# A new order of jobs on five engine queues, and other engines for some copies, squares and evacuations, in a gated recurrence fused with a feed-forward network

## The chip, the cores and the metric

The kernel runs on one core of a Trainium2 chip. The metric is the device time of one execution in microseconds (us); the runs shown give their median. The core has a matrix engine (PE, TensorE), three engines for elementwise work (VectorE or DVE, ScalarE or ACT, GpSimd or POOL) and a queue (SP) that issues the transfers. Each engine works through its own queue strictly in order and waits, through semaphores, for what its next instruction needs.

## The reference

A gated linear recurrence over 4 sequences of 5824 steps with 256 channels, and a feed-forward network on each of the 23296 tokens that it gives:

```python
sig_r = 1.0 / (1.0 + np.exp(-r_gate)); sig_i = 1.0 / (1.0 + np.exp(-i_gate))
log_a = c * sig_r * np.log(np.clip(a_base, 1e-06, 1.0 - 1e-06))[None, None, :]
a_t = np.exp(log_a)
norm = np.sqrt(np.maximum(1.0 - a_t * a_t, 1e-06))
x_gated = norm * sig_i * x
for t in range(S):
    h = a_t[:, t] * h + x_gated[:, t]
    y[:, t] = h
...
a = x @ w1          # x is y, 23296 x 256; w1, w2: 256 x 1024
b = x @ w2
h = a * b @ w3      # w3: 1024 x 1024
return (h @ w_out)  # w_out: 1024 x 256
```

## The kernel before

The tokens are cut into 47 chunks: 0 and 1 of 256 tokens, 2 to 45 of 512, and 46 of 256. The product of `w3` and `w_out` is formed once at the start, so that a chunk needs three matrix products: two up (256 to 1024) and one down (1024 to 256). The recurrence needs channels on the partitions and time along the row, so the gates are turned, in some chunks by PE, in the others by a transposing transfer.

Each chunk is a set of small jobs, and the program is one string, `ORDER`, of job names. A loop reads it word by word and calls the function that emits the job's instructions. Each engine's queue is therefore the string without the jobs of other engines; no scheduler moves anything afterwards. Eight sets of numbers (`DV_COPY`, `AC_SQUARE` and so on) say on which engine a copy, square, cast or evacuation is emitted. The buffers are rings: a job that takes the next buffer of a ring waits for the reader of its former content. The product `a` and the down product share a ring of four PSUM buffers.

The jobs, with `c` the chunk, and in brackets engine and line of the profile:

- `r i x`: loads of the two gates and of x (SP, L151); `L` and `C`: load and cast of a piece of a weight (L407; L414 or L416)
- `R I`: tanh of the gates (ACT, L160 to L168); `p`, `t`: gate plus one, and its product with x, the tile `u_t`, in two halves (POOL, or DVE at L189 or L192)
- `V U`: the turning of both (PE, L200, or SP, L211)
- `d`: exp, the decay `a_t`, one job for each half of the channels (ACT, L223); `s`: its square, into `nrm` (POOL or DVE L233, ACT L231); `q`: root (ACT, L238); `g`: product with the turned `u_t` (DVE, L248 or L251)
- `h`: the scan, one for each half of the channels (DVE, L270); `y`: cast to bf16 (POOL, L282)
- `a`, `b`: the up products into the tiles `pa` and `pb` (PE, L299). `a7.3.0` is chunk 7, group 3 of 4, first half; `b7.3` is both halves
- `c`: copy of `pa` from PSUM to `sa` (ACT L322 or DVE L320); `m`: product of `sa` and `pb` into `g_t` (DVE, L337)
- `D`: down product of 128 tokens, 8 matmuls over the groups of `g_t` in their order, into `po` (PE, L357); `e`: its evacuation to `ot` (ACT L322 or DVE L320); `o`: store (SP)
- `Ft Fc Fm Fe`: the forming of `w3` times `w_out`: turning (PE, `ptw`), copy of `ptw`, product (PE, `pw`), evacuation of `pw` (DVE L472 or ACT)
- `W`: two matmuls without use, to keep PE active (L287); `E`, `A`: small preparations.

A chunk's chain is loads, `R I`, `V U`, `d s q g`, `h`, `y`, `a b`, `c`, `m`, `D`, `e`, `o`. The recurrence of a chunk is computed some chunks ahead of its matrix products.

```python
    def copy_to(dve, dst, src_ps):
        if dve:
            nc.vector.tensor_copy(out=dst, in_=src_ps)
        else:
            nc.scalar.copy(out=dst, in_=src_ps)
...
    for word in ORDER.split():
        name, args = re.fullmatch(r"([LC]w[123o]\.|A\d\.|[A-Za-z]+)([\d.]*)", word).groups()
        steps[name](*(int(v) for v in args.split(".") if v))
```

Of the kernel before, what the change touches and what calls it, by code (L numbers as in the profile page):

```python
# [23 lines left out]
def kernel(  # L24
# [150 lines left out]
    def times(c, half):  # L175
# [49 lines left out]
    def square(c, cb):  # L225
# [6 lines left out]
        else:  # L232
            (nc.vector if (c, cb) in DV_SQUARE else nc.gpsimd).tensor_mul(out=n, in0=a, in1=a)  # L233

# [37 lines left out]
    def cast(c, cb=None):  # L272
# [8 lines left out]
        else:  # L281
            (nc.vector if key in DV_CAST else nc.gpsimd).tensor_copy(out=y, in_=h)  # L282

# [190 lines left out]
    def last(c):  # L474
# [33 lines left out]
        I7 I8 D0.1 D0.0 b3.0 b3.1 a3.1.0 g4 h4.0 h4.1 s5.1 R8 R9 d6.0 d6.1 p6 y4 p8 t5.0 t5.1 D0.3 D0.2 m3.0 e0.0
# [156 lines left out]
```

## Time and profile before

| what | before |
|---|---|
| time of the runs shown | 511.43 us median (511.33, 511.43, 511.6) |
| span of the profiled execution | 509.1 us (its own time is not listed; the median of the runs is 2.3 us above its span) |
| PE busy | 501.7 us, 99% of the span, 3225 matmuls |
| ScalarE busy | 461.5 us, 91% |
| VectorE busy | 431.8 us, 85% |
| GpSimd busy | 318.0 us, 62% |
| moved by transfers | 124.06 MB, mean 244 GB/s |
| granted PE clock | 1.000 |

Busy times are unions of the instructions' intervals. Matmuls overlap one another, so a matmul is read by the distance from its start to the next start and not by its length. An engine's row in the order of time gives start and length of a run of equal instructions, their count behind the x, and in brackets how long the engine stood idle before it and what ended that.

### The profile page before, as it was taken

Reading aid. Unit: us, or ns where it says so; the run is one execution under the profiler, and the core shown is the slowest. Engines: PE = TensorE matmul, PEld = TensorE weight load, DVE = VectorE, ACT = ScalarE, POOL = GpSimd, SP = SyncE. Lnnn points to the kernel's source line nnn. Section 1 sums busy time; section 2 is a strip of 40 time slices with the busy share of each in tenths; the row PEclk is TensorE's granted clock in tenths of the full one; section 3 lists DMA queues with packets and bytes.
Section 4 is the critical chain, followed back from the end, with each engine's and each line's share of the span. In section 5 each row is a group of like instructions: output and inputs, shape, how many; then the busy total and the mean of one; then the engine's idle time right before and its main releaser. Section 6 shows DMA issues by size and latency. Waiting matters only on the chain.

```text
span 509.1 us, 8891 instructions
## 1 busy us (share of the span) xinstructions
PE 501.7 (99%) x3225; PEld 308.3 (61%) x3225; DVE 431.8 (85%) x417; ACT 461.5 (91%) x708; POOL 318.0 (62%) x269
## 2 busy tenths in 40 slices
PE   7999999999999999999999999999999999999997
PEld 3767665665665656556656556565566655656566
DVE  6999999999999789879979799878877797959762
ACT  7999999998999999999999999998998979888543
POOL 1686677658658937964886973956647568580200
PEclk9999999999999999999999999999999999999999
DMA  8999999999989998896999997899886895252213
GB/s 317 410 411 345 335 316 282 305 286 259 310 220 298 279 285 247 211 302 196 247 305 327 254 286 148 252 243 227 210 246 164 235 298 161 85 166 62 65 51 104
DMA packets 178048, 124.06 MB, mean 244 GB/s; under 512 B 87378, under 2 KB 174036, under 8 KB 178004
## 3 DMA queue, kind: packets, MB, share of 16 engines
q1 hardware_dynamic: 178000, 123.50, 85.4%
q8 instruction: 25, 0.41, 0.4%
q14 instruction: 19, 0.16, 0.1%
q10 hardware_dynamic: 4, 0.00, 0.0%
HBM read 78.91 MB, written 23.86 MB: 202 GB/s over the span
## 4 chain that ended last, share of the span: by engine, by line
PE 92%; ACT 3%; DMA 2%; POOL 1%; DVE 1%; issue 1%; SPq 1%; ACTq 0%; DVEq 0%
PE po L357 30%; PE pb L299 29%; PE pa L299 29%; DMA wf<-in_moe_w_dram 2%; PE pw L436 1%; ACT sa L322 1%; PE ptr L200 1%; PE ptw L425 1%; POOL u_t L192 0%; DVE h_t L270 0%; SPq L151 0%; ACT ot L322 0%; SPq L407 0%; ACT L168 0%; ACT L238 0%
## 5 line engine op out<-in xcount | busy, mean ns | idle before, releaser
L337 DVE TENSOR_TENSOR g_t<-sa,pb 128x1024 bf16<-128x1024 bf16 (+1 forms) x188 | 218.7, 1180 | 58.9 <-PE pb L299 27.6
L299 PEld LDWEIGHTS <-w_sb 128*128 128x128 bf16 x1504 | 146.4, 98 | 144.1 <-issue 1.4
L322 ACT CAST sa<-pa 128x512 bf16<-128x512 f32 (+1 forms) x332 | 179.8, 591 | 27.1 <-PE pa L299 18.9
L299 PE MATMUL pa<-y_t,w_sb 128*128 128x512 bf16 (+1 forms) x752 | 190.2, 372 | 0.2 <-ACT sa L322 0.2
L299 PE MATMUL pb<-y_t,w_sb 128*128 128x512 bf16 (+1 forms) x752 | 184.9, 372 | 0.2 <-ACT w_sb L414 0.2
L357 PE MATMUL po<-wp_sb,g_t 128*128 128x256 bf16 (+1 forms) x1464 | 177.6, 272 | 0.0
L357 PEld LDWEIGHTS <-g_t 128*128 128x128 bf16 x1464 | 142.5, 98 | 39.5 <-issue 0.3
L282 POOL CAST y_t<-h_t 128x1024 bf16<-128x1024 f32 (+2 forms) x47 | 53.8, 1145 | 140.2 <-DVE h_t L270 136.1
L192 POOL TENSOR_TENSOR u_t<-i_t,x_t 128x512 bf16<-128x512 f32 (+1 forms) x90 | 123.3, 1387 | 3.8 <-DMA ut<-u_t 1.8
L270 DVE TENSOR_TENSOR_SCAN h_t<-a_t,h_t,nrm 128x512 f32<-128x512 f32 (+1 forms) x92 | 121.1, 1343 | 1.6
L233 POOL TENSOR_TENSOR nrm<-a_t 128x512 f32<-128x512 f32 x70 | 78.4, 1137 | 7.0 <-ACT a_t L223 4.0
L223 ACT ACTIVATE a_t<-rt,la 128x512 f32<-128x512 bf16 (+1 forms) x82 | 66.1, 823 | 0.0
L322 ACT COPY ot<-po 128x512 f32<-128x512 f32 x84 | 49.1, 589 | 13.2 <-PE po L357 12.9
L173 POOL TENSOR_SCALAR i_t<-i_t 128x1024 f32<-128x1024 f32 (+1 forms) x45 | 55.4, 1233 | 8.3 <-ACT i_t L168 8.3
L251 DVE SCALAR_TENSOR_TENSOR nrm<-nrm,ut 128x1024 f32<-128x1024 f32 (+1 forms) x39 | 53.2, 1365 | 5.2 <-ACT nrm L238 5.2
L168 ACT ACTIVATE i_t<-i_t 128x1024 f32<-128x1024 f32 (+1 forms) x46 | 48.5, 1063 | 0.3 <-DMA i_t<-in_i_gate_dram 0.2
L238 ACT ACTIVATE nrm<-nrm 128x1024 f32<-128x1024 f32 (+1 forms) x47 | 48.4, 1040 | 0.2
L162 ACT ACTIVATE th_r<-r_t 128x1024 bf16<-128x1024 f32 (+1 forms) x41 | 43.5, 1064 | 0.0
L320 DVE CAST sa<-pa 128x512 bf16<-128x512 f32 x36 | 23.5, 684 | 1.4 <-PE pa L299 0.8
L238 ACT ACT_TABLE_LOAD x17 | 21.8, 1283 | 0.4
L287 PE MATMUL warm<-ident 128*128 128x512 bf16 x32 | 10.7, 473 | 1.6 <-DVE ident L441 1.6
L231 ACT ACTIVATE nrm<-a_t 128x512 f32<-128x512 f32 x18 | 11.4, 645 | 0.0
(55 smaller groups left out, 122.1 us busy)
## 6 DMA issues: line engine op xcount, KB each, us to landing
r_t<-in_r_gate_dram SPq DMA_DIRECT2D x45, 512.0 KB, 5.2
i_t<-in_i_gate_dram SPq DMA_DIRECT2D x45, 512.0 KB, 6.0
x_t<-in_x_dram SPq DMA_DIRECT2D x45, 512.0 KB, 5.5
out_dram<-ot SPq DMA_DIRECT2D x90, 256.0 KB, 3.9
wf<-in_moe_w_dram SPq DMA_DIRECT2D x12, 512.0 KB, 10.5
wf<-in_moe_w_out_dram SPq DMA_DIRECT2D x2, 512.0 KB, 10.2
rt<-th_r SPq DMA_TRANSPOSE x41, 4.7
ut<-u_t SPq DMA_TRANSPOSE x39, 4.4
```

The source lines that it names most:

```text
L173: (nc.vector if c in DV_PLUS else nc.gpsimd).tensor_scalar(t, t, 1.0, 1.0, op0=ALU.add, op1=ALU.mult)
L192: (nc.vector if (c, half) in DV_HALF else nc.gpsimd).tensor_mul(out=u, in0=t, in1=xt)
L223: nc.scalar.activation(out=a, in_=pr, func=AF.Exp, scale=la4[:, cb:cb + 1], bias=la4[:, cb:cb + 1])
L233: (nc.vector if (c, cb) in DV_SQUARE else nc.gpsimd).tensor_mul(out=n, in0=a, in1=a)
L238: nc.scalar.activation(out=n, in_=n, func=AF.Sqrt, scale=-1.0, bias=1.0)
L251: nc.vector.scalar_tensor_tensor(out=n, in0=n, scalar=1e-3, in1=T["pu", c][:, :, cols], op0=ALU.max, op1=ALU.mult)
L270: nc.vector.tensor_tensor_scan(h[:, cb, :], a[:, cb, :], n[:, cb, :], init, ALU.mult, ALU.add)
L282: (nc.vector if key in DV_CAST else nc.gpsimd).tensor_copy(out=y, in_=h)
L299: nc.tensor.matmul(out=dst, lhsT=w_sb[:, cb, m * P:(m + 1) * P], rhs=T["y", gates_of(c)][:, cb, span(c, mp)], start=(cb == 0), stop=(cb == ...
L322: nc.scalar.copy(out=dst, in_=src_ps)
L337: nc.vector.tensor_mul(out=T["g", z][:, 2 * mp:2 * mp + 2, span(c, mp)], in0=T["sa", c, mp][:, :, :w], in1=T["pb", c, mp][:, :, :w])
L357: nc.tensor.matmul(out=po, lhsT=T["g", c][:, k, j * P:(j + 1) * P], rhs=wp_sb[:, k, cols], start=(k == 0), stop=(k == KD - 1), skip_group_ ...
```

## The change

All five queues get a new order up to about chunk 26; from there on the string is the old one word for word (PE from `a26.3.1`, VectorE from `h28.0`, ScalarE from `c26.3.0`, GpSimd from `s31.1`, SP from `o24.0`). The jobs are the same; the transposes that PE makes, the ring sizes and the number of warming matmuls stay. These jobs change their engine:

| job | before | after |
|---|---|---|
| copies `c` on VectorE (others ScalarE) | 36, all up to chunk 12 | 70: 37 up to chunk 12, 33 later |
| evacuations `e` on VectorE | 7 | 11: 5 up to chunk 12, 6 later |
| squares `s` on ScalarE | 18 | 29 |
| squares `s` on GpSimd | 70 | 59 |
| second product `t` of a half on VectorE (others GpSimd) | 0 | 3 |
| whole cast `y` on ScalarE (others GpSimd) | 0 | 2 |
| fold copies `Fc` and evacuations `Fe` on VectorE | 8 and 4 | 7 and 6 |
| weight cast `Cw1.1` | VectorE | GpSimd |
| cast of chunk 1 on VectorE and ScalarE | `y1.1` and `y1.0` | `y1.0` on VectorE, none on ScalarE |

```diff
-    DV_HALF = set()
-    DV_SQUARE = {(0, 0), (0, 1), (5, 1), (9, 0)}
+    DV_HALF = {(9, 1), (16, 0), (30, 1)}
+    DV_SQUARE = {(0, 0), (0, 1), (7, 0), (26, 1)}
...
-    DV_CAST = {(1, 1)}
-    AC_CAST = {(1, 0)}
+    DV_CAST = {(1, 0)}
+    AC_CAST = {22, 24}
...
-    DV_EVAC = {(0, 0), (0, 1), (4, 1), (5, 1), (6, 1), (9, 0), (9, 1)}
-    FOLD_ACT = {('e', 0), ('e', 4), ('e', 5), ('e', 7)}
+    DV_EVAC = {(0, 0), (0, 1), (4, 0), (5, 0), (7, 0), (14, 1), (17, 0), (19, 1), (20, 0), (22, 0), (23, 0)}
+    FOLD_ACT = {('c', 7), ('e', 6), ('e', 7)}
...
-    W_ACT = {('w2', 0), ('w3', 3)}
-    W_DVE = {('w1', 1)}
+    W_ACT = {('w2', 0), ('w3', 5)}
+    W_DVE = set()
...
     ORDER = """
-        r0 i0 x0 Lw1.1 Lw1.0 r2 i2 Lw2.0 Lw3.2 x2 E W13 A3. A0. A1. A2. R0.1 R0.0 W3 W10 V0.0 V0.1 I0 t0.1 d0.0 s0.0
+        r0 E W0 A3. A0. A1. A2. W11 W1 R0.1 V0.1 W7 i0 R0.0 V0.0 I0 x0 W3 t0.0 d0.1 Lw1.1 d0.0 Lw1.0 W4 W15 t0.1
...
-        a7.0.1 b7.1 c7.3.0 R15 c7.0.0 c7.0.1 D6.0 D6.1 a7.3.1 D5.0 D6.2 b7.3 D6.3 D5.1 d11.1 c7.3.1 e6.0 s11.1 I12
+        m7.1 p11 o4.0 r15 x12 r17 h8.0 d11.0 D6.1 h8.1 a7.3.1 D6.0 e6.0 c7.3.1 a7.0.0 c7.0.0 b7.3 o6.0 m7.3 D6.3
```

In the last pair of lines PE's jobs are, before, `b7.1 D6.0` with `a7.0.0 a7.0.1` ahead of them, and after, `b7.1` (on the line ahead) and `D6.1` with `a7.0.0` behind.

The first place is the start of VectorE's queue, from the products of chunk 0 (`u_t`) and squares (`nrm<-a_t`) through the first gatings (`nrm<-nrm,ptr`) and scans (`h_t`) to the first copies (`sa`) and products (`g_t`). Before:

```order
L189 SCALAR_TENSOR_TENSOR u_t_157<-i_t_99,x_t_101 128x512
L233 TENSOR_TENSOR nrm_161<-a_t_159 128x512 x2
L189 SCALAR_TENSOR_TENSOR u_t_157<-i_t_99,x_t_101 128x512
L416 CAST w1_sb_90<-wf_103 128x2x512
L248 SCALAR_TENSOR_TENSOR nrm_161<-nrm_161,ptr_182 128x256 x2
L270 SCALAR_TENSOR_TENSOR h_t_214<-a_t_159,nrm_161 128x256 x2
L248 SCALAR_TENSOR_TENSOR nrm_161<-nrm_161,ptr_182 128x256 x2
L270 SCALAR_TENSOR_TENSOR h_t_214<-a_t_159,h_t_214,nrm_161 128x256 x2
L282 CAST y_t_217<-h_t_214 128x256
L320 CAST sa_271<-pa_220 128x2x256
L320 CAST sa_273<-pa_223 128x2x256
L337 TENSOR_TENSOR g_t_278<-sa_271,pb_266 128x2x256
```

And the same stretch after:

```order
L194 SCALAR_TENSOR_TENSOR u_t_149<-i_t_135,x_t_144 128x512 x2
L238 TENSOR_TENSOR nrm_184<-a_t_151 128x512 x2
L253 SCALAR_TENSOR_TENSOR nrm_184<-nrm_184,ptr_169 128x256 x2
L275 SCALAR_TENSOR_TENSOR h_t_193<-a_t_151,nrm_184 128x256 x2
L253 SCALAR_TENSOR_TENSOR nrm_184<-nrm_184,ptr_169 128x256 x2
L275 SCALAR_TENSOR_TENSOR h_t_193<-a_t_151,h_t_193,nrm_184 128x256 x2
L287 CAST y_t_212<-h_t_193 128x256
L325 CAST sa_246<-pa_241 128x2x256
L325 CAST sa_259<-pa_250 128x2x256
L342 TENSOR_TENSOR g_t_268<-sa_259,pb_261 128x2x256
L342 TENSOR_TENSOR g_t_268<-sa_246,pb_272 128x2x256
```

Both products now come ahead of the squares, the weight cast (`w1_sb`) is gone, and a second product follows the first two copies.

The second place is VectorE around the last product of chunk 6 (`m6.3`), the one into `g_t_1291` with `pb_1335` before and into `g_t_1289` with `pb_1347` after. Before:

```order
L320 CAST sa_1320<-pa_1288 128x512
L320 CAST sa_1320<-pa_1270 128x512
L337 TENSOR_TENSOR g_t_1291<-sa_1320,pb_1315 128x1024
L337 TENSOR_TENSOR g_t_1291<-sa_1259,pb_1327 128x1024
L320 CAST sa_1358<-pa_1324 128x512
L337 TENSOR_TENSOR g_t_1291<-sa_1358,pb_1335 128x1024
L251 SCALAR_TENSOR_TENSOR nrm_1224<-nrm_1224,ut_1294 128x1024
L270 SCALAR_TENSOR_TENSOR h_t_1364<-a_t_1137,h_t_1187,nrm_1224 128x512 x2
```

After:

```order
L342 TENSOR_TENSOR g_t_1289<-sa_1228,pb_1257 128x1024
L325 COPY ot_1304<-po_1267 128x512
L325 CAST sa_1309<-pa_1291 128x512
L325 CAST sa_1309<-pa_1294 128x512
L342 TENSOR_TENSOR g_t_1289<-sa_1309,pb_1299 128x1024
L342 TENSOR_TENSOR g_t_1289<-sa_1244,pb_1311 128x1024
L325 CAST sa_1323<-pa_1317 128x512
L342 TENSOR_TENSOR g_t_1289<-sa_1323,pb_1347 128x1024
L256 SCALAR_TENSOR_TENSOR nrm_1265<-nrm_1265,ut_1231 128x1024
L256 SCALAR_TENSOR_TENSOR nrm_1336<-nrm_1336,ut_1234 128x1024
```

The rows around `m6.3` stay, an evacuation (`ot`) stands among them, and two gatings follow in place of one and a pair of scans.

The third place is VectorE between two scans of chunk 20, where it has products only before:

```order
L270 SCALAR_TENSOR_TENSOR h_t_2866<-a_t_2353,h_t_2790,nrm_2417 128x512
L337 TENSOR_TENSOR g_t_2899<-sa_2870,pb_2860 128x1024
L337 TENSOR_TENSOR g_t_2899<-sa_2826,pb_2909 128x1024
L337 TENSOR_TENSOR g_t_2899<-sa_2904,pb_2920 128x1024
L270 SCALAR_TENSOR_TENSOR h_t_2866<-a_t_2353,h_t_2790,nrm_2417 128x512
```

And after:

```order
L275 SCALAR_TENSOR_TENSOR h_t_2910<-a_t_2349,h_t_2811,nrm_2432 128x512
L325 CAST sa_2924<-pa_2895 128x512
L342 TENSOR_TENSOR g_t_2898<-sa_2917,pb_2912 128x1024
L342 TENSOR_TENSOR g_t_2898<-sa_2864,pb_2942 128x1024
L325 CAST sa_2924<-pa_2948 128x512
L325 CAST sa_2965<-pa_2973 128x512
L342 TENSOR_TENSOR g_t_2998<-sa_2924,pb_2982 128x1024
L275 SCALAR_TENSOR_TENSOR h_t_2910<-a_t_2349,h_t_2811,nrm_2432 128x512
```

Three copies from PSUM (`sa<-pa`) that ScalarE made before now stand between the scans.

More of the change, by code (lines that the diff above doesn't have):

```diff
@@ new lines @@
+        a24.2.0 c24.0.1 a24.3.1 b24.0 s28.0 a24.2.1 c24.2.0 y25 a25.0.1 m24.0 D23.1 c24.3.1 c24.2.1 b24.2
+        a24.3.0 D23.0 h26.0 h26.1 c25.0.1 e23.0 V29 s28.1 q28 c24.3.0 D22.3 m24.2 b24.3 i31 a25.1.1 a25.2.0
+        a25.0.0 d32.1 s32.1 I32 D22.2 c25.1.1 b25.0 e22.1 a25.1.0 c25.0.0 m24.3 t27.1 t27.0 U27 c25.2.0 y26 g27
+        c25.1.0 d32.0 D23.3 a26.0.0 r33 d29.0 o23.0 s29.0 p30 t30.1 p29 r37 m25.0 D23.2 b25.1 m25.1 a25.2.1 r36
+        c25.2.1 x29 e23.1 V31 a26.1.0 R34 x32 c26.0.0 i34 b25.2 m25.2 a26.0.1 d29.1 s29.1 c26.1.0 h27.0 a25.3.1
@@ L631 @@
+        b46.1 c46.0.1 c46.2.1 a46.1.1 D45.0 D45.1 c46.1.1 m46.0 e44.1 m46.1 b46.2 a46.3.1 a46.3.0 b46.3 D45.2
+        D45.3 e45.0 c46.3.0 c46.3.1 o44.0 o45.0 e45.1 o44.1 o45.1 m46.2 m46.3 D46.0 D46.1 e46.0 e46.1 o46.0
+        o46.1
         """
```

274 lines of the change are left out of this document (138 added, 136 removed), and 10 rows, old and new, of the table DV_COPY.

## The prediction

> **What bounds the kernel now.** I read the page's busy shares first, then the sums by stage, then the waits, then single rows in order of time. The sums by stage (columns: stage, length, then busy microseconds and count of PE, weight load, VectorE, ScalarE and GpSimd, granted clock, DMA share, GB/s):
>
> ```profile
> 0.00:20.00 20.00, 16.01 (x99) 8.70 (x99) 14.24 (x36) 16.71 (x21) 7.33 (x14) 1.00 0.92 349
> 20.00:60.00 40.00, 39.91 (x329) 27.89 (x330) 39.29 (x54) 39.53 (x55) 29.56 (x29) 1.00 1.05 377
> 60.00:100.00 40.00, 40.00 (x267) 24.91 (x265) 39.14 (x39) 39.91 (x61) 26.25 (x22) 1.00 1.07 299
> 100.00:140.00 40.00, 40.00 (x245) 23.78 (x244) 39.45 (x42) 37.43 (x56) 28.77 (x22) 1.00 1.09 288
> 140.00:200.00 60.00, 60.00 (x370) 36.07 (x369) 53.21 (x46) 57.92 (x90) 41.76 (x33) 1.00 0.96 271
> 200.00:250.00 50.00, 50.00 (x307) 29.81 (x305) 43.59 (x37) 49.45 (x77) 33.88 (x29) 1.00 0.88 244
> 250.00:300.00 50.00, 50.00 (x310) 30.16 (x309) 41.64 (x32) 48.87 (x76) 40.90 (x33) 1.00 1.07 281
> ```
>
> PE is full from 20 us on, and up to 140 us VectorE is full too: 117.88 of 120 us, so 1.8% idle. Only after 140 us has VectorE air: 21.56 of 160 us. A busy PE may still be a slow PE, so I look at its pace in the chain that ended last (start, length, what):
>
> ```profile
> 117.94 1.02 PE pb L299 x4
> 131.52 1.73 PE pb L299 x8
> 141.94 1.75 PE po L357 x16
> 236.38 1.00 PE pb L299 x4
> ```
>
> Eight matmuls of 512 columns take 1.73 us, four therefore 0.87, and one of 256 columns takes 1.75 / 16 = 0.109. The fours at 117.94 and 236.38 lose 0.15 and 0.13. Read in the same way, the largest later stall is here (start, length, instruction, idle before and who ended it):
>
> ```profile
> 366.99 1.03 PE L299 MATMUL pa<-y_t,w_sb 128*128 128x512 bf16 x4
> 368.20 0.59 PE L299 MATMUL pa<-y_t,w_sb 128*128 128x512 bf16 x2 [0.18 <-ACT sa L322]
> ```
>
> From 366.99 to 368.20 are 1.21 us for four, 0.34 too many. These three make 0.62; with smaller ones I estimate 1.0 us of stalls after 90 us. That is all that a better order can win there, since the change leaves PE's matmuls the same in number and size. The rest of what can be won lies in the start:
>
> ```profile
> 13.11 1.04 PE L299 MATMUL pa<-y_t,w_sb 128*128 128x256 bf16 x8
> 15.22 0.61 PE L299 MATMUL pb<-y_t,w_sb 128*128 128x256 bf16 x4 [0.19 <-ACT w_sb L414]
> 26.38 1.02 PE L299 MATMUL pa<-y_t,w_sb 128*128 128x512 bf16 x4
> ```
>
> The first useful group starts at 13.11; at 26.38 chunk 2 starts, after about 10 us of useful matmuls in 13.3 us.
>
> **The change part by part.** *Start.* The rows of VectorE that carry it, and two of ScalarE, before:
>
> ```profile
> 7.08 0.69 DVE L189 SCALAR_TENSOR_TENSOR u_t<-i_t,x_t 128x512 bf16<-128x512 f32 x1 [1.62 <-DMA x_t<-in_x_dram]
> 7.69 1.29 DVE L233 TENSOR_TENSOR nrm<-a_t 128x512 f32<-128x512 f32 x2
> 8.89 0.69 DVE L189 SCALAR_TENSOR_TENSOR u_t<-i_t,x_t 128x512 bf16<-128x512 f32 x1
> 9.49 0.69 DVE L416 CAST w_sb<-wf 128x1024 bf16<-128x1024 f32 x1
> 10.36 0.75 DVE L248 SCALAR_TENSOR_TENSOR nrm<-nrm,ptr 128x256 f32<-128x256 f32 x2 [0.18 <-PE ptr L200]
> 17.35 0.69 DVE L320 CAST sa<-pa 128x512 bf16<-128x512 f32 x1 [0.79 <-PE pa L299]
> 22.73 2.49 DVE L270 TENSOR_TENSOR_SCAN h_t<-a_t,h_t,nrm 128x512 f32<-128x512 f32 x2
> 25.72 0.41 DVE L472 TENSOR_SCALAR wp_sb<-pw 128x256 bf16<-128x256 f32 x1
> 27.44 1.99 DVE L320 CAST sa<-pa 128x512 bf16<-128x512 f32 x3
> 9.31 1.15 ACT L238 ACTIVATE nrm<-nrm 128x512 f32<-128x512 f32 x2
> 11.77 1.06 ACT L160 ACTIVATE th_r<-r_t 128x1024 bf16<-128x1024 f32 x1
> ```
>
> Now both `u_t` products stand ahead of the two squares and the weight cast is gone to GpSimd. `x_t` still releases the first at 7.08. Four operations at 0.60 from start to start (7.08 to 7.69 to 8.89) put the last square at 8.89 to 9.58, so ScalarE's root, half of 1.15 long, starts at 9.6 (9.31 before), ends at about 10.2 and the gating starts at 10.25 where it was 10.36. The 0.61 us of the cast become idle time in front of it. Behind it the order is tighter: two products now follow the first two copies, which covers part of the 0.79 us. Walking on with the same lengths I get the copy of chunk 1 at 17.3 (17.35 before) and the scan of chunk 2 at 22.1 (22.73), of which 0.61 is the missing cast, and which a copy that comes to VectorE (`c1.2.0`, 0.60) takes back before 27.44. So beyond its load VectorE gains 0.15 us; the bounds are -0.3 (the transpose of `u_t` now waits behind eight warming matmuls and could end after the root) and +0.9 (both stalls, 0.18 and 0.79, gone). PE itself starts later, as `V2` and two more warming matmuls now stand before its first group: ScalarE's `R2`, from 11.77 to 12.83 before, comes 0.3 later with the root and ends near 13.1, so the group starts near 14.0 in place of 13.11, but fewer holes follow, and PE could reach chunk 2 about 1 us earlier if VectorE's `h2`, and with it `y2`, allowed it.
>
> The Trainium skill ("TensorE: Matmul & The Clock Gate", What's actually happening) says that PE runs at half rate until one window of some 3.4 us has been busy. By it the eight warming matmuls could end as late as an estimated 10.1 us, which would lean to the lower bound. The sum does not use it.
>
> *Chunks 2 to 8.* VectorE is full here, so its position is its load. Its queue ahead of the last product of chunk 6 (`m6.3`) is compared job by job: it gains 2 copies (0.60 each) and 2 evacuations of the folded weights (0.41 long at 25.72, 0.34 each without the overlap), and loses one `ptw` copy (0.60) and the weight cast (0.61); squares and halves cancel. Net +0.67 us. PE has less ahead of its first `D` of chunk 6: two groups `a` of 0.43, 0.87 us, now come after it. Both ends of this meeting before:
>
> ```profile
> 87.52 0.69 DVE L320 CAST sa<-pa 128x512 bf16<-128x512 f32 x1
> 88.34 1.22 DVE L337 TENSOR_TENSOR g_t<-sa,pb 128x1024 bf16<-128x1024 bf16 x1
> 89.48 1.22 DVE L251 SCALAR_TENSOR_TENSOR nrm<-nrm,ut 128x1024 f32<-128x1024 f32 x1
> 89.12 1.03 PE L299 MATMUL pb<-y_t,w_sb 128*128 128x512 bf16 x4
> 89.98 1.91 PE L357 MATMUL po<-wp_sb,g_t 128*128 128x256 bf16 x16
> ```
>
> `m6.3` ends at 89.56. The seventh of eight matmuls is the first to read it, at 89.98 + 6 x 0.109 = 90.63: 1.07 us to spare. After: `m6.3` ends at 89.56 + 0.67 - 0.15 = 90.1, and PE without a stall is there at 90.63 - 0.87 = 89.76. PE waits, and is then 0.4 us (0.35 and a semaphore) later in its work than before, whatever it won at the start. With the bounds above: -0.35 to +0.85. That is the term that decides against a gain. The copies that ScalarE loses, and casts, squares and halves that GpSimd loses or gets in this stretch, cost nothing here: ScalarE was waited for rarely (0.8 us by VectorE between 26 and 160 us), and GpSimd itself waits most:
>
> ```profile
> DVE g_t L337 <- ACT sa L322: 0.8, 3, 0.3
> POOL y_t L282 <- DVE h_t L270: 136.1, 36, 10.3
> ```
>
> If that cover went, `y` would be late next and PE would stand in front of an `a`.
>
> *Chunks 9 to 26.* Here 33 copies and 6 evacuations go from ScalarE to VectorE, and 2 halves of `u_t` and a square from GpSimd to it. Over the whole prefix VectorE has 34 copies, 4 evacuations and 3 halves more (41 x 0.60), the two losses above (1.21) less and the two folds (0.68) more: +24.1 us, nearly all after 120 us. From there the order is old again; the first old row of VectorE is `h28.0`, and right ahead of it stands `m25.3`, which PE's `D25` reads:
>
> ```profile
> 296.26 2.19 DVE L270 TENSOR_TENSOR_SCAN h_t<-a_t,h_t,nrm 128x512 f32<-128x512 f32 x1
> 294.88 1.91 PE L357 MATMUL po<-wp_sb,g_t 128*128 128x256 bf16 x16
> ```
>
> VectorE came to `h28.0` at 296.26 having idled, from 20 us on, 2.1 + 6.8 + 6.4 + 8.4 = 23.7 us (the stages above; in the last one 8.4 of 50 lie before 296.26, as it is busy from there to 300). With 24.1 more, and 0.15 won at the start, it comes there at 296.5 if no idle time at all is left, and `D25` needs `m25.3` at 294.88 + 0.65 = 295.5. So it would be 1.0 us late, plus its idle time i, less what it saves elsewhere. i: the full stretch had 1.8%, which on 275 us is 4.9. The saving r is in scans and gatings that run beside GpSimd (two queries, the scans of L270 and the gatings of L251, one row each from the full and the loose stretch):
>
> ```profile
> 60.00:140.00 80.00, 21.25 (x17) 1.00 1.08 294
> 200.00:300.00 100.00, 28.88 (x20) 1.00 0.98 263
> 60.00:140.00 80.00, 9.86 (x8) 1.00 1.08 294
> 200.00:300.00 100.00, 12.92 (x9) 1.00 0.98 263
> ```
>
> A scan takes 1.25 us in the full stretch and 1.44 in the loose one, a gating 1.23 and 1.44; 20 x 0.19 + 9 x 0.21 make 5.7 us, and I take 6.5 with the stage before, as the upper end of r; the lower end is 0. Lateness is 1.0 + 4.9 - r, from -0.6 to 5.9. I take -0.6, no stall: VectorE will be as full there as it was before 140 us, and in that regime GpSimd stood waiting for the scan and did not run against it. The rule in the Trainium skill ("SBUF — State Buffer", Who interferes with whom) is that a VectorE operation with two SBUF inputs and a GpSimd operation that reads SBUF exclude each other, whoever starts second waiting for the whole other one. The longer scans agree; by it alone r would only shrink with GpSimd's own work, for an estimated lateness near 5 us and a time near 516.5 us.
>
> *Tail.* From chunk 27 on all five queues are in the old order, so the end costs what it did.
>
> *Sum.* The profiled span is 509.1 us; the median 511.43 is 2.3 more for what lies around it, which I keep. 0.4 us at chunk 6, of the later stalls about half gone (-0.3), as much new ones of the same kind (+0.4): span 509.6, time 511.9. By 0.2%, or 1.0 us, a measurement of this kernel can be told from no change, so this counts as the same.
>
> **Rivals.** *VectorE is the bound at chunk 25* (slower): r stays near 3, because GpSimd still runs into the scans. Then PE passes `D25` 2.9 us later than before, the 0.4 of chunk 6 included: 511.4 + 2.9 + 0.1 (the later stalls as in the sum) = 514.4 us. It is slower as soon as r is below 5.0 (lateness 0.9), and without any saving 517.4. For it speak the 24.1 us against 23.7; against it the 120 us in which PE never waited for a VectorE that was as full.
>
> *The start pays after all* (faster): VectorE loses neither 0.18 nor 0.79, so PE is 0.35 earlier at chunk 6, and the 1.0 us of later stalls go because ScalarE has 38 copies less to make: 511.4 - 0.4 - 1.0 = 510.0. Against it: `x_t`, two products, two squares and a root stand in a row before the first gating, and none of them got shorter.
>
> *The change moves work only where nothing waits:* PE stays at its pace and chunk 6 is met in time, 511.4. It lies within the likeliest case.
>
> **How the numbers follow.** About the same, 511.9 with its own range 510.5 to 512.4: 0.47. Slower by over 0.2%: 0.39, of which 0.30 is the bound at chunk 25 and 0.09 other new waits of an order that leaves VectorE no air. Faster by over 0.2%: 0.14. The range reaches from the faster rival, 510.0, to just past the slower one, 514.6, and leaves out some 5% below and 12% above.
>
> **What would show it.** Right: the first group `pa` near 14.0; VectorE's first gating near 10.25 and its scan of chunk 2 near 22; `m6.3` ending near 90.1 with a stall of PE in the first `po` group of chunk 6; VectorE at 97% or more from 140 to 295 us, its scans there at 1.25 us. Wrong: a gap of over 1 us on PE before `D25` with `m25.3` ending after 296 (the slower rival), `m6.3` before 89.5 (the faster one), or a wait of PE for a transfer, for which no row of before speaks.

## The result: 0.5% slower

The changed kernel takes 514.15 us (median of 5 runs, 512.9 to 514.43), the kernel before 511.43 us beside it (5 runs, 511.29 to 511.87): 1.0051 times as long, 95% interval 1.0039 to 1.0063. The time lies in the forecast range (510.0 to 514.6), but the case that was held likeliest, no change at 511.9, did not come. The profiled execution took 514.15 us with a span of 512.3 us. Its sums by stage, in the columns of the first table of the prediction:

```profile
0.00:20.00 20.00, 15.49 (x110) 8.94 (x111) 14.34 (x35) 16.47 (x21) 9.95 (x16) 1.00 0.91 347
20.00:60.00 40.00, 38.78 (x311) 26.17 (x312) 39.67 (x54) 38.66 (x53) 29.27 (x28) 1.00 1.04 358
60.00:100.00 40.00, 39.74 (x267) 25.32 (x270) 39.49 (x42) 38.04 (x55) 23.06 (x20) 1.00 1.10 317
100.00:140.00 40.00, 37.90 (x220) 21.57 (x223) 37.84 (x40) 37.35 (x55) 31.07 (x26) 1.00 1.15 268
140.00:200.00 60.00, 59.62 (x367) 36.40 (x373) 58.69 (x58) 56.07 (x84) 36.67 (x31) 1.00 1.05 277
200.00:250.00 50.00, 49.73 (x303) 29.85 (x305) 48.26 (x50) 45.91 (x67) 24.39 (x21) 1.00 0.99 256
250.00:300.00 50.00, 49.51 (x308) 30.43 (x312) 49.01 (x48) 46.03 (x70) 27.87 (x22) 1.00 0.90 261
```

VectorE is now full to 300 us (155.96 of 160 us after 140, against 138.44 before), and ScalarE has air. Most of PE's new idle time lies between 100 and 140 us (37.90 of 40, where before had 40.00). Some 53 matmul records are missing from this trace, so small gaps of PE count for nothing here; I therefore measure PE by its *lag*: for each down product, its start less the length, at PE's pace, of all the matmuls that stand ahead of it, and that figure less the same one of the kernel before. At 100 us of PE's own work the lag is 0.21 us, at 120 it is 2.34, at 275 it is 2.58, at 300 it is 3.23, and 3.26 at the end. So the loss is made in two places, one large and one small, and the tail, in the old order, adds nothing.

The large one, in order of time: SP's issue of `V13`, the transposing transfer of chunk 13; ScalarE's rows at its landing; PE's rows; a pair of scans on VectorE:

```profile
102.80 6.40 SPq L216 DMA_TRANSPOSE rt<-th_r  x1
114.98 0.81 ACT L228 ACTIVATE a_t<-rt,la 128x512 f32<-128x512 bf16 x1 [2.38 <-DMA rt<-th_r]
115.70 0.56 ACT L327 COPY ot<-po 128x512 f32<-128x512 f32 x1
112.61 1.45 PE L304 MATMUL pa<-y_t,w_sb 128*128 128x512 bf16 x5 [0.50 <-DVE ot L325]
113.90 1.03 PE L304 MATMUL pb<-y_t,w_sb 128*128 128x512 bf16 x4
116.32 1.10 PE L304 MATMUL pa<-y_t,w_sb 128*128 128x512 bf16 x4 [1.39 <-ACT ot L327]
108.62 3.35 DVE L275 TENSOR_TENSOR_SCAN h_t<-a_t,h_t,nrm 128x512 f32<-128x512 f32 x2
```

and the same in the chain of waits:

```profile
102.80 12.16 DMA rt<-th_r
```

`V13` is issued at 102.80 and lands 12.16 us later. `d13.0` stands at ScalarE's head and waits 2.38 us for it; behind it stands `e7.1`, an evacuation that has nothing to do with chunk 13, and PE waits for the PSUM buffer that `e7.1` frees: four matmuls from 113.90 should end at 114.77, the next start at 116.32. The issue of `V13` itself keeps SP for 6.40 us (1.31 us for the transposing transfer at 99.17, ahead of the loads), so all that SP issues behind it comes later too. The 0.50 us at 112.61 are another wait, for an evacuation on VectorE that stands behind the pair of scans: the pair took 3.35 us, beside a GpSimd product, and 2.46 in the second profile of this program, which has no such wait. The whole-kernel list of waits has two rows that before had not:

```profile
ACT a_t L228 <- DMA rt<-th_r: 2.5, 2, 2.4
PE pa L304 <- ACT ot L327: 1.4, 1, 1.4
```

In the transfer view of 100 to 116 us (0.4 us a number) the queue stands almost still from 109.2 to 112.8 us while `V13` is under way:

```profile
GB/s 387 379 389 331 292 286 349 356 315 295 261 274 246 328 366 361 361 379 382 387 353 252 172 13 3 8 10 26 23 26 23 23 140 345 248 323 358 325 219 42
```

The small one, at chunk 25, is a single scan. VectorE's and GpSimd's rows there:

```profile
288.11 1.27 POOL L197 TENSOR_TENSOR u_t<-i_t,x_t 128x512 bf16<-128x512 f32 x1
288.21 2.25 DVE L275 TENSOR_TENSOR_SCAN h_t<-a_t,h_t,nrm 128x512 f32<-128x512 f32 x1
```

GpSimd's product starts 0.10 us ahead of the scan `h27.0`, and the scan takes 2.25 us in place of 1.26.

### The profile page after: what moved, and what is told of

It is laid out like the page before. It is cut to its first block, busy times and chain, and to the rows that moved or that the text cites. A ratio compares the mean times of both kernels' runs of the same rounds, so it can differ in the third digit from the quotient of the medians.

```text
span 512.3 us, 8861 instructions
## 1 busy us (share of the span) xinstructions
PE 498.6 (97%) x3172; PEld 307.1 (60%) x3225; DVE 450.3 (88%) x458; ACT 453.2 (88%) x681; POOL 295.7 (58%) x255
## 4 chain that ended last, share of the span: by engine, by line
PE 83%; DMA 4%; DVE 4%; ACT 4%; issue 3%; SPq 1%; POOL 0%; DVEq 0%; ACTq 0%
PE po L362 28%; PE pb L304 27%; PE pa L304 26%; DMA rt<-th_r 2%; DMA wf<-in_moe_w_dram 2%; DVE g_t L342 2%; ACT sa L327 1%; PE pw L441 1%; DVE h_t L275 1%; SPq L156 1%; PE ptr L205 1%; ACT ot L327 1%; PE ptw L430 1%; ACT a_t L228 0%; DVE sa L325 0%
## 5 line engine op out<-in xcount | busy, mean ns | idle before, releaser
L327 ACT CAST sa<-pa 128x512 bf16<-128x512 f32 (+1 forms) x298 | 162.4, 586 | 31.8 <-PE pa L304 21.0
L304 PE MATMUL pa<-y_t,w_sb 128*128 128x512 bf16 (+1 forms) x719 | 185.7, 372 | 3.7 <-ACT ot L327 1.4
L287 POOL CAST y_t<-h_t 128x1024 bf16<-128x1024 f32 (+2 forms) x46 | 48.9, 1065 | 155.7 <-DVE h_t L275 150.1
L197 POOL TENSOR_TENSOR u_t<-i_t,x_t 128x512 bf16<-128x512 f32 (+1 forms) x87 | 119.0, 1383 | 3.3 <-DMA x_t<-in_x_dram 1.5
L275 DVE TENSOR_TENSOR_SCAN h_t<-a_t,h_t,nrm 128x512 f32<-128x512 f32 (+1 forms) x92 | 117.9, 1313 | 1.2
L238 POOL TENSOR_TENSOR nrm<-a_t 128x512 f32<-128x512 f32 (+1 forms) x59 | 66.0, 1133 | 21.5 <-ACT a_t L228 14.3
L327 ACT COPY ot<-po 128x512 f32<-128x512 f32 x80 | 46.3, 584 | 15.8 <-PE po L362 15.7
L256 DVE SCALAR_TENSOR_TENSOR nrm<-nrm,ut 128x1024 f32<-128x1024 f32 (+1 forms) x39 | 50.4, 1296 | 4.2 <-ACT nrm L243 4.0
L325 DVE CAST sa<-pa 128x512 bf16<-128x512 f32 x70 | 46.2, 678 | 0.8 <-PE pa L304 0.2
L236 ACT ACTIVATE nrm<-a_t 128x512 f32<-128x512 f32 x29 | 18.3, 634 | 0.1
```

Source lines behind the costliest of these rows:

```text
L256: nc.vector.scalar_tensor_tensor(out=n, in0=n, scalar=1e-3, in1=T["pu", c][:, :, cols], op0=ALU.max, op1=ALU.mult)
L275: nc.vector.tensor_tensor_scan(h[:, cb, :], a[:, cb, :], n[:, cb, :], init, ALU.mult, ALU.add)
L304: nc.tensor.matmul(out=dst, lhsT=w_sb[:, cb, m * P:(m + 1) * P], rhs=T["y", gates_of(c)][:, cb, span(c, mp)], start=(cb == 0), stop=(cb == ...
```

## Experiments

The lags of all profiles, by PE's own work in us (the trace's time is 8 to 15 us more). Between the columns stand the start (50), the transfers of chunks 13 and 16 (100 to 120), smaller waits behind them (120 to 150), chunk 21 (220 to 250), chunk 25 (275 to 300). e6 stands for e6_d13_d16_later, and so on; the order lines shown are pieces of `ORDER`:

```
kernel                    50    100    120    150    220    250    275    300    480
after                   0.39   0.21   2.34   2.43   2.46   2.58   2.58   3.23   3.26
e9_after_again          0.36   0.18   0.59   1.16   1.19   2.17   2.17   2.82   2.82
e10_after_third         1.34   1.16   2.17   2.74   2.77   3.75   3.75   4.40   4.40
e1_d13_later            0.21   0.03  -0.12  -0.14  -0.11   0.88   0.88   1.52   1.53
e2_v13_early            0.35   0.17   1.72   2.30   2.33   3.31   3.31   3.96   3.97
e5_fetch_shift          1.79   1.61   1.45   1.43   1.46   1.59   1.59   2.24   2.27
e6_d13_d16_later        0.16  -0.02  -0.17   0.46   0.49   1.48   1.48   2.14   2.17
e11_e6_again            0.27   0.09  -0.07   0.56   0.58   0.70   0.70   1.35   1.39
e12_scan_alone          0.62   0.44   0.29   0.91   0.94   1.07   1.07   1.60   1.64
e7_copies_back          0.12  -0.06  -0.22   0.43   0.46   4.55   4.55   6.02   6.05
e8_before_dve_load      0.06   4.30   4.30   4.30   4.30   4.33   4.33   4.33   4.37
```

**e1_d13_later: is it `d13.0` at ScalarE's head?**

```diff
-c9.0.1 e7.0 d13.0 b8.1 m8.1 D7.3 b9.0 m9.0 t13.0 V16 D7.2 e7.1 a8.3.1 c8.3.1 o7.1 i15 a9.1.1 d13.1
+c9.0.1 e7.0 b8.1 m8.1 D7.3 b9.0 m9.0 t13.0 V16 D7.2 e7.1 a8.3.1 c8.3.1 o7.1 i15 a9.1.1 d13.0 d13.1
```

> The changed kernel with one word moved: the job d13.0 (ScalarE's exp for chunk 13, which stood 2.38 us waiting for the transposing transfer of chunk 13) now stands directly ahead of d13.1, behind the evacuation e7.1 and the copy c8.3.1. Theory A (the late transfer, through ScalarE's queue, costs PE 2.1 us near 113 us): ScalarE reaches e7.1 without the wait, PE's stall near 113 to 116 us goes, span near 510.2, time near 512.1. Theory B (VectorE's load is what PE lacks; a stall removed at 113 us comes back at a later meeting): the lag of PE behind the kernel before is 3.2 us again from chunk 25 on, time near 514.

Measured: 513.78 us (median of 10 runs, 512.39 to 516.12), ratio 1.0045 (1.0029 to 1.0061). In its profile, which is its fastest run, the loss at chunk 13 is gone (lag -0.12 after it). But `V13` landed at 111.75 there, before ScalarE would have come to `d13.0` in its old place (112.3), so this profile does not show that the edit helps against a late landing; e12, further down, does. The median fell by less than 0.4 us, so in other runs the time goes elsewhere, and 0.99 us appear at chunk 21 that the first profile of the changed kernel did not have.

**e2_v13_early: is it the place of `V13` in SP's queue?** `V13` was moved ahead of four loads:

```diff
-a8.0.0 c7.0.1 m7.0 x13 s11.1 m7.2
+a8.0.0 c7.0.1 m7.0 V13 x13 s11.1 m7.2
...
-m8.0 t11.1 V13 q11 i16 U11
+m8.0 t11.1 q11 i16 U11
```

> The changed kernel with one word moved: the transposing transfer V13 is issued ahead of the loads x13, i14, x14 and r14 instead of behind them. Theory A: it lands before 107 us in place of 114.96, ScalarE does not wait for it, and PE's stall near 113 us goes: time near 512.1. If instead a transposing transfer that meets a pause of the transfer queue is late wherever it stands, and the pause at 108 to 113 us comes again, then one of the four loads behind it is late by some 4 us, and the time stays above 513. Theory B: near 514.

Measured: 514.59 us (4 runs, 513.82 to 515.06), ratio 1.0057 (1.0040 to 1.0074). `V13` now lands 3.81 us after its issue. `U11`, the transposing transfer that now stands right behind the loads, lands 11.64 us after its own, and its issue keeps SP for 6.48 us: what is late is whichever of them stands there. `V16`, issued behind it, brings the same kind of wait back (chain of waits, then ScalarE and PE):

```profile
112.50 5.80 DMA rt<-th_r
118.32 0.82 ACT L228 ACTIVATE a_t<-rt,la 128x512 f32<-128x512 bf16 x1 [1.95 <-DMA rt<-th_r]
119.66 0.59 PE L304 MATMUL pa<-y_t,w_sb 128*128 128x512 bf16 x2 [1.54 <-ACT sa L327]
```

So moving one transfer does not help: the loads hold up the next one, and ScalarE's order leaves no time between a landing and its use, with PSUM copies queued behind it.

**e3_old_engines and e4_new_engines: the two halves of the change apart.** The first has the new `ORDER` with the old sets of engines, the second the old `ORDER` with the new sets; nothing else differs.

> The new order of jobs with the old sets, so that copies, squares, casts, evacuations and halves run on the engines of the kernel before. VectorE has 24 us less up to chunk 26, ScalarE 10 us more. Theory A (order decides: the place of V13): the wait near 113 us stays, and the 0.6 us at chunk 25 go; time near 513.5. Theory B (VectorE's load decides): near 511.5 to 512. As the order was made for other engines, new waits of some us on ScalarE are possible too: then above 514.

> The old order of jobs with the new sets of engines. Theory A: the transfers keep their old places, no wait for V13, so only new waits of VectorE, which has 24 us more up to chunk 26 in an order not made for it: 511.5 to 513. Theory B (VectorE's load decides): VectorE reaches its scan of chunk 28 late and PE stalls at chunk 25 and ahead of it: 513 to 516.

Measured: 559.89 us (4 runs, ratio 1.0949, 1.0917 to 1.0980) and 563.66 us (4 runs, 1.1019, 1.0991 to 1.1047). Neither number expected was near. PE's waits of the second kernel, and of the first:

```profile
PE pb L304 <- DVE g_t L342: 12.1, 12, 4.3
PE po L357 <- ACT sa L322: 7.4, 7, 2.5
```

Each half by itself costs some 50 us and the two together 2.7. Their mean granted clock was 0.988 and 0.982, so by an estimate from these means 7 and 10 us of it are PE at a lower clock, and the rest is waits. An order is made for the engines that its jobs run on: with other sets a copy stands on its engine behind jobs that were meant to be elsewhere. The halves cannot be added, so this pair tells that they belong together, and nothing on how the 2.7 us divide.

**e5_fetch_shift: does an instruction fetch make `V13` late?** In the first profile a 16 KB instruction packet is moved at 109.08 us, where the pause begins. Cutting warm-up matmuls in quarters shifts all later fetches:

```diff
+            for k in range(4 if i in QUARTERED else 1):
+                n = CT // P // (4 if i in QUARTERED else 1)
...
+    QUARTERED = {0, 11, 1, 7, 3}
```

> The changed kernel, with the filler matmuls of five warm-up steps cut in four quarters each, at the start where PE waits anyway: 60 instructions more on PE, so that each later 16 KB instruction fetch comes some 5.6 us earlier (109.1 to about 103.5). Theory (the transposing transfer V13 is late because an instruction fetch falls into it): V13 lands by 111, ScalarE does not wait for it, PE's lag at 110-120 us falls from 2.1 to under 0.5 us, time 512.2 to 512.8. Rival (V13 is late because four loads stand ahead of it in the transfer queue): V13 lands at 114 to 115 again, 514.2.

Measured: 513.69 us (4 runs, 512.88 to 514.59), ratio 1.0050 (1.0036 to 1.0065). The packet is at 104.29, `V13` lands 8.8 us after its issue at 104.3, and nothing is lost at chunk 13. But `V13` takes 8.1 to 9.4 us in e1, e6, e7, e9 and e11 too, with the fetch still at 108 to 109, and a short pause of the queue is there in e5 without a fetch (26 GB/s at 111.2 us). So the fetch is not shown to be the cause; what is shown is that the four loads ahead of `V13` cost it some 5 us (3.81 without them in e2), and in the first profile, with the long pause, it took some 3 us more. The time did not fall because PE lost 1.4 us at the start, and so this run does not test the wait at chunk 13 either: all that needs `V13` came 1.4 us later. What PE lost it lost to its clock. PE's rows there, and the stage in the columns of the first table (in the changed kernel the same eight matmuls take 0.62 us from 13.21 and the first six `pa` 0.82 from 14.10):

```profile
12.94 1.00 PE L206 MATMUL ptr<-ident,th_r 128*128 128x128 bf16 x8 [2.02 <-ACT th_r L166]
14.59 1.49 PE L307 MATMUL pa<-y_t,w_sb 128*128 128x256 bf16 x6
13.00:16.40 3.40, 3.40 (x18) 2.20 (x19) 2.39 (x4) 3.38 (x5) 2.48 (x3) 0.50 1.03 416
```

The granted clock is 0.50 for these 3.4 us, right behind PE's wait of 2.02 us, and 1.00 before and after.

**e9_after_again, e10_after_third: how much of it recurs?** The changed kernel, as it is.

> The changed kernel as it is, for a second profile. Theory (the long pause of the transfers at 109 to 113 us recurs in most runs and makes V13 late by 1 to 3 us): V13 lands at 113.5 to 115.5, PE's lag of some 2 us at 110-120 us is there again, 514 to 514.5. Rival (the pause falls now here, now there): V13 lands by 112.5 as in the kernels with edits, and the lag comes at other places or not at all, 512.5 to 514.5. In both the 0.5 us at chunk 25 are there again.

> The same kernel, for a third profile; the same numbers as for the second.

Measured: 513.69 and 515.27 us (one run each, before 511.43 beside them). `V13` lands 9.37 and 10.11 us after its issue (12.16 in the first), and between 100 and 120 us 0.41 and 1.01 us are lost (2.13 in the first). But it is the next transfer, `V16`, that costs them. ScalarE does not wait for `V13` at all in the second profile, and for 0.32 us in the third, which costs PE 0.14. `V16`, whose issue stands behind the long ones of `V13` and `U11`, is waited for at `d16.0`; ScalarE and PE in the second profile:

```profile
117.19 0.81 ACT L228 ACTIVATE a_t<-rt,la 128x512 f32<-128x512 bf16 x1 [0.81 <-DMA rt<-th_r]
118.53 0.59 PE L304 MATMUL pa<-y_t,w_sb 128*128 128x512 bf16 x2 [0.41 <-ACT sa L327]
```

In the third the two waits are 0.99 and 0.79 us. Chunk 21 costs 0.98 us in both, 0.12 in the first; chunk 25 costs 0.65 us in all three. In the third the start costs 1.34 us: its first product starts at 7.61 (7.11 in the first) and PE waits 0.26 us more for a weight. The rival comes nearer: the loss falls now here, now there, at places that are the same few each time.

**e6_d13_d16_later and e11_e6_again: both transfers' users moved back.** As e1, and `d16.0` likewise:

```diff
-c8.3.0 R14 b9.1 d16.0 c9.1.1 m9.1
+c8.3.0 R14 b9.1 c9.1.1 m9.1
...
-t12.1 h11.0 h11.1 d16.1 a10.0.1
+t12.1 h11.0 h11.1 d16.0 d16.1 a10.0.1
```

> The changed kernel with d13.0 and d16.0 directly ahead of d13.1 and d16.1 on ScalarE, so that no evacuation that PE waits for stands behind a transposing transfer of chunks 13 and 16. Theory (these two waits are the loss at 110-120 us, and which of the two is hit varies from run to run): no lag there in any run, median 512.7 to 513.0 with the 1.6 us of chunks 21 and 25 left, and less spread than the 3.7 us of the kernel with d13.0 alone moved. Rival (other transfers are hit in their turn): median 513.6 or above, spread as before.

> The changed kernel with d13.0 and d16.0 moved, as before, for a second profile. Theory (what is left is VectorE in chunks 21 and 25 and short transfer waits that vary): lag of 1.0 to 1.6 us between 230 and 297 us again, 0 to 1.5 us elsewhere, at another place than the 0.65 us at 130-140 us of the first profile. Rival (the rest is fixed by the order): 0.65 us at 130-140 us again, total within 0.2 us of 2.2.

Measured: 513.5 us (6 runs, 512.17 to 514.67), ratio 1.0042 (1.0029 to 1.0056); 512.26 us in the second profile. Nothing is lost between 100 and 120 us in either profile. But the median is higher than the theory had it, and the second profile loses 1.39 us in all, so the rival's fixed 2.2 falls too. What is left, first, is 0.63 us between 120 and 150 us in both. The edit makes it. The wait of 0.65 us is at the same `pa` in all four profiles with `d16.0` moved (e6, e7, e11, e12) and in none without. ScalarE and PE in e6:

```profile
117.78 1.07 ACT L327 CAST sa<-pa 128x512 bf16<-128x512 f32 x2 [1.07 <-DVE g_t L342]
142.48 1.54 ACT L327 COPY ot<-po 128x512 f32<-128x512 f32 x3
143.58 0.59 PE L304 MATMUL pa<-y_t,w_sb 128*128 128x512 bf16 x2 [0.49 <-ACT ot L327]
```

In e1 `d16.0` ran in the wait ahead of the two copies, of which 0.30 us were left. In e6 ScalarE stands idle there and makes up for `d16.0` later. It has no idle time from there until 143 us, so its three evacuations start at 142.48 (141.81 in e1), and PE waits. What is left, second, is 0.65 us at chunk 25 in both, and at chunk 21 0.99 us in the first profile and 0.12 in the second, though the kernel is the same. The two rows that differ there, VectorE's pair of scans and GpSimd's operation; first e6_d13_d16_later:

```profile
232.70 3.32 DVE L275 TENSOR_TENSOR_SCAN h_t<-a_t,h_t,nrm 128x512 f32<-128x512 f32 x2
233.91 1.05 POOL L178 TENSOR_SCALAR i_t<-i_t 128x1024 f32<-128x1024 f32 x1 [2.46 <-ACT i_t L173]
```

then e11_e6_again:

```profile
232.79 2.46 DVE L275 TENSOR_TENSOR_SCAN h_t<-a_t,h_t,nrm 128x512 f32<-128x512 f32 x2
234.00 2.09 POOL L178 TENSOR_SCALAR i_t<-i_t 128x1024 f32<-128x1024 f32 x1 [2.47 <-ACT i_t L173]
```

The second scan of the pair and GpSimd's `p24` start within 0.01 us of each other, and one of them takes twice its time: the scan (2.12, `p24` 1.05) or `p24` (2.09, the scan 1.26). All nine profiles of the new order but e3 and e7 fit: `h22.1` took 2.0 to 2.1 us in e1, e2, e6, e9 and e10, where chunk 21 costs 0.98 or 0.99, and 1.26 us in the first profile, e5, e11 and e12, where it costs 0.12 or 0.13.

**e7_copies_back: is VectorE's load the cause at chunks 21 and 25?**

On top of e6, which the expectation below calls the kernel before; the second line is in words:

```diff
-    DV_COPY = {... (21, 0, 0), (21, 2, 1), (25, 3, 1), (26, 2, 0) ...}
+    DV_COPY without these four
```

> The kernel before with four copies given back from VectorE to ScalarE: c21.0.0, c21.2.1, c25.3.1, c26.2.0. Theory (VectorE, full, delays PE in chunks 21 and 25, while ScalarE stands idle there): the 1.6 us of lag at 230-297 us falls to under 0.4, median 511.2 to 511.8, no slower than the kernel before the change. Rival (ScalarE has no room for 2.3 us): time as without it, 512.7 to 513, or longer.

Measured: 517.61 us (4 runs, 516.93 to 517.97), ratio 1.0121 (1.0108 to 1.0135): 4.1 us above e6, against the theory and far more than the rival had. ScalarE's, VectorE's and PE's rows, and a stage behind them:

```profile
238.43 1.07 ACT L327 CAST sa<-pa 128x512 bf16<-128x512 f32 x2 [2.49 <-DVE g_t L342]
235.97 2.35 DVE L342 TENSOR_TENSOR g_t<-sa,pb 128x1024 bf16<-128x1024 bf16 x2 [0.85 <-PE pb L304]
239.56 1.66 PE L362 MATMUL po<-wp_sb,g_t 128*128 128x256 bf16 x8 [2.29 <-ACT sa L327]
239.80:243.20 3.40, 3.40 (x14) 1.65 (x12) 0.17 (x1) 3.37 (x5) 2.65 (x3) 0.50 1.12 263
```

`c21.2.1` needs one of the three `sa` buffers, and the product that frees it ends at 238.3, as in e11, where VectorE makes the copy. On VectorE the copy waits without harm, since the product is ahead of it in the same queue; on ScalarE it holds up everything behind it for 2.49 us, and PE for 2.29. The rest of the 4 us at chunk 21 is the clock: behind this wait it was granted at 0.50 for 3.4 us, and 14 matmuls that take 2.2 us at PE's pace took 3.84. So not all of the 4.1 us speaks against the theory, but the wait alone cost more than the 1.6 us that the theory could have won there and at chunk 25: the idle time of ScalarE there was no room for a copy.

**e8_before_dve_load: has VectorE air before chunk 6?** The kernel before, the edit in words:

```diff
+    DV_COPY also has (4, 2, 0), (4, 3, 0), (5, 1, 1)
```

> The kernel before the change, with three more copies of chunks 4 and 5 on VectorE (c4.2.0, c4.3.0, c5.1.1), 1.8 us of load. Theory (VectorE is the bound up to chunk 6 with little air, as the prediction's second step has it): PE is 1.0 to 1.6 us late from chunk 6 on, 512.4 to 513.0. Rival (VectorE has air there): 511.4.

Measured: 516.48 us (6 runs, 515.18 to 517.71), ratio 1.0100 (1.0084 to 1.0116). 1.8 us of load cost 4.3 us of lag, more than either theory said. VectorE and PE:

```profile
62.42 2.46 DVE L271 TENSOR_TENSOR_SCAN h_t<-a_t,h_t,nrm 128x512 f32<-128x512 f32 x2
64.80 1.26 DVE L321 CAST sa<-pa 128x512 bf16<-128x512 f32 x2
65.52 0.59 PE L300 MATMUL pa<-y_t,w_sb 128*128 128x512 bf16 x2 [2.78 <-DVE sa L321]
```

On VectorE `c4.2.0` stands behind a pair of scans, and PE needs the buffer that it frees: the price is the place in the queue (2.78 us, and 0.6 behind it for an evacuation on VectorE), not the 0.6 us of the copy. So this run says that VectorE has no free place there, but not how much load it could bear in the right one.

**e12_scan_alone: the scans freed of GpSimd.** On top of e6, four jobs are moved, none added (GpSimd's own order changes at `t30.0` alone; `p24` comes later because it waits for `I24`):

```diff
-h22.1 a20.3.1 I24 d26.0 a21.1.0 b21.0 t25.0 c20.3.1 p24 i27 t24.0 e18.1 x26
+h22.1 a20.3.1 d26.0 a21.1.0 b21.0 t25.0 c20.3.1 i27 e18.1 I24 p24 t24.0 x26
...
-b26.0 t30.0 m26.0
+b26.0 m26.0
...
-y27 b26.1
+y27 t30.0 b26.1
```

> The kernel with d13.0 and d16.0 moved, and two GpSimd operations taken away from beside a scan: I24 (and p24 and t24.0 behind it) behind e18.1, so that p24 no longer starts together with h22.1, and t30.0 behind y27, so that it no longer runs at the start of h27.0. No operation is added, removed or changed. Theory (the losses at chunks 21 and 25 are single scans that wait for GpSimd, 2.1 and 2.25 us in place of 1.26): h22.1 and h27.0 take 1.2 to 1.3 us, the lag that grows by 0.98 or 0.1 us at 220-250 us grows by 0.1 there and the 0.65 us at 270-290 us fall to at most 0.2; span 509.8 to 510.2, median 511.8 to 512.6. Rival (VectorE's load as such holds PE there, and it loses the microsecond elsewhere): the 0.5 us before 290 us stay, 513 to 513.5.

Measured: 512.5 us (11 runs, 512.28 to 513.87), ratio 1.0025 (1.0016 to 1.0034), 1.0 us below e6 with less spread. VectorE, then the rows at 297 to 302 us of GpSimd, ScalarE and PE:

```profile
286.70 1.28 DVE L275 TENSOR_TENSOR_SCAN h_t<-a_t,h_t,nrm 128x512 f32<-128x512 f32 x1
296.33 2.41 DVE L275 TENSOR_TENSOR_SCAN h_t<-a_t,h_t,nrm 128x512 f32<-128x512 f32 x1
297.63 1.95 POOL L238 TENSOR_TENSOR nrm<-a_t 128x512 f32<-128x512 f32 x1
299.61 1.06 ACT L243 ACTIVATE nrm<-nrm 128x1024 f32<-128x1024 f32 x1 [0.82 <-POOL nrm L238]
301.19 1.08 PE L304 MATMUL pa<-y_t,w_sb 128*128 128x512 bf16 x4 [0.30 <-ACT ot L327]
```

`h22.1` takes 1.26 us and chunk 21 costs 0.13, which e11 had without the move. `h27.0` takes 1.28 us and the loss before 290 us is gone; in all nine profiles of the new order without the move, e3 left out, it took 2.25. Half a microsecond then appears at 300 us: the product that was moved delays GpSimd's square `s31.1`, the root waits for that, and an evacuation that PE needs stands behind the root. So the theory is shown for `h27.0` and agrees with `h22.1`, and its span (510.7, against 509.8 to 510.2) is missed by the new wait and a start that lost 0.6 us in this run. This profile also shows what the moved exponentials are worth: `V16` landed at 118.13, 1.55 us after ScalarE came to the old place of `d16.0`, and PE lost nothing there. None of the versions beats the kernel before.

## Why the prediction was right and wrong

*Start: sizes right.* VectorE's and PE's rows in the changed kernel:

```profile
10.30 0.75 DVE L253 SCALAR_TENSOR_TENSOR nrm<-nrm,ptr 128x256 f32<-128x256 f32 x2 [0.70 <-ACT nrm L243]
22.39 2.45 DVE L275 TENSOR_TENSOR_SCAN h_t<-a_t,h_t,nrm 128x512 f32<-128x512 f32 x2
13.21 0.62 PE L205 MATMUL ptr<-ident,th_r 128*128 128x128 bf16 x8 [2.09 <-ACT th_r L165]
14.10 0.82 PE L304 MATMUL pa<-y_t,w_sb 128*128 128x256 bf16 x6
```

First gating 10.30 (forecast 10.25), scan of chunk 2 at 22.39 (22.1), first group 14.10 (near 14.0). The lower bound, transposes of `u_t` that end behind the root, did not come: the eight warming matmuls ended at 7.9 us, and in the third profile, where they ended latest, at 9.8 us, the transposes were still done 0.5 us before the root let the gating start. The start differs by up to 1.2 us from run to run (0.12 to 0.62 us of lag in most profiles, 1.34 in one), which no term held.

*Chunk 6: size right, place not.* `m6.3` was forecast to end at 90.1 with a stall in the first down product:

```profile
88.75 1.22 DVE L342 TENSOR_TENSOR g_t<-sa,pb 128x1024 bf16<-128x1024 bf16 x1 [0.30 <-PE pb L304]
89.35 1.06 PE L362 MATMUL po<-wp_sb,g_t 128*128 128x256 bf16 x8
```

It ended at 89.97 and the seventh matmul read it at 89.35 + 0.65 = 90.00: met, with nothing to spare. PE was 0.21 us late there (0.4 forecast, -0.35 to 0.85), from the start and not from a stall.

*Chunks 9 to 26: no stall by load, as taken; but single scans.* The forecast was that VectorE comes to `h28.0` at 296.5 if it loses all its idle time. In e12, with every job on the same engine, it is there at 296.33, so the load does fit. The saving was mis-sized. The rows of the scans of the changed kernel in the two stretches that the prediction used, then those of the gatings:

```profile
60.00:140.00 80.00, 19.85 (x15) 1.00 1.13 293
200.00:300.00 100.00, 25.87 (x19) 1.00 0.94 259
60.00:140.00 80.00, 8.46 (x7) 1.00 1.13 293
200.00:300.00 100.00, 12.24 (x10) 1.00 0.94 259
```

A gating now takes 1.21 and 1.22 us, as forecast, but a scan 1.32 and 1.36, not 1.25: GpSimd still runs into some of them. From 200 to 300 us that saves some 3.7 us of the forecast 5.7, which is nearer to the slower rival's r. The rule that was weighed (the Trainium skill, "SBUF — State Buffer", Who interferes with whom: whoever issues first holds the shared ports for its whole instruction, and the other waits) agrees with the pairs at 233.9 and 288.1 us: GpSimd's length and a scan's 1.26 make the time to the scan's end within 0.2 us. Which of the two goes first is not always the one that starts first: `h28.0` in e12, at 296.33 us, waits for a GpSimd product that starts 0.07 us after it, right behind another GpSimd operation. As an average, 516.5, the rule was too dear, since most scans run alone; as an event it cost 0.98 us in two profiles of three, 0.65 in all three and 0.50 in the first, at chunk 13. One step that failed is the reading of r as a mean over scans: what counts is whether the one scan that PE waits behind is hit.

*The largest loss was in no term.* This is the other step that failed: the term for new waits. The prediction held that the copies that leave ScalarE "cost nothing here" and priced new small waits at 0.4 us; the wait for a transfer alone cost 1.55 us in the first profile. It looked at loads of engines, not at transfers, and named "a wait of PE for a transfer, for which no row of before speaks" as what would prove it wrong. A row of before could have spoken: `V13` landed there at 107.9 us and the first exponential of chunk 13, there `d13.1`, started at 110.2, 2.3 us later, with `e7.1` another 2.9 us behind. The change put four loads in place of one directly ahead of `V13`, which lands 7.1 us later, and `e7.1` directly behind the exponential, to which ScalarE comes 2.4 us later. With the same wait for `V16` this cost 1.6, 0.4 and 1.0 us in three profiles, and the moved exponentials of e6 and e12 remove it, at the price of 0.65 us elsewhere.

*The slower rival* gave 514.4 us, near the 514.15 measured, but by luck, since its place was wrong: of its 2.9 us at chunk 25 0.65 were found, and they were a collision and not a lack of idle time. That the time lies in the range is luck in the same way, as the upper end was drawn from this rival. *The faster one*: before loses 0.12 to 0.15 us each at 86.5, 117.9 and 236.4 us; e12 loses nothing at these matmuls, but new stalls outweigh them. The largest of the stalls that the prediction added up, 0.34 us at 368 us, could not go: it lies in the tail, whose order is the old one, and e1 has it again (0.34 at 369.7). *Tail*: unchanged, as forecast (3.23 at 300 us of work, 3.26 at the end).

## What to carry to other kernels

Where engines run fixed queues, a new order is judged by the margins between a landing or a release and the instruction that waits for it, and by what stands behind that instruction on its engine; sums of load per engine say whether the work fits, and little about who waits, once two engines are full. One 0.6 us copy given to another engine held PE up for 2.3 us in e7 and 2.8 us in e8, as its place there was behind other work or a wait. Moving a job out of the way can also take it out of a gap that it filled, as `d16.0` did in e6. And a kernel with no margin has to be profiled more than once: here three profiles of one program lost their microseconds in three mixes of the same few places.

## What the hardware showed that was not expected

- Two instructions of VectorE and GpSimd that start 0.01 us apart exclude each other, and which of the two waits changes from one execution to the next (the rows at 233.9 us); PE's lag at chunk 21 moves by 0.87 us with it.
- The transfer queue can stand almost still for 3.6 us (3 to 26 GB/s from 109.2 to 112.8 us) with a transposing transfer of 256 B packets under way, and then go on at 345 GB/s. In other profiles of the same program the pause at this place is about 1 us, and the kernel before has such a one too (2 and 9 GB/s in two slices of 0.5 us from 106.5 us). A fetch of instructions falls near it, but moving the fetch did not settle whether it is the cause; that is open.
- A gap of PE can cost twice, once as a wait and once as half clock behind it. The granted clock changes at multiples of 3.41 us after its first change. In such windows PE stood idle for 59% (e5, up to 13.01 us) and 67% (e7, up to 239.81), and the clock was 0.50 in the window behind them, where PE lost 1.4 and 1.6 us. With e3 and e4 there are eight such falls before the end of a kernel, all behind windows with 56.9% idle or more; of the other windows at full clock only one lies above that (57.5%, in e4). The changed kernel's 2.09 us of waiting at 11 to 13 us stay below that, with at most 49% idle in one window, because they fall into two windows.
- At the very start the clock column reads 1.00, but PE runs at half pace: four warming matmuls of 512 columns take 1.89 us at 2.78, and at 6.00 eight do. In the third profile of the same program the eight still take 2.99 us, from 6.85.
